# A recurrence with experts behind it: the state products of a chunk's output issued as one run, the score products as another, and a planner's table of deadlines replaced

## The chip, the cores and the metric

The kernel runs on one core of one Trainium2 chip. The metric is the device time of one execution in microseconds (us); smaller is better. The kernel before takes 564.5 us (median of three runs, 563.0 to 564.85).

Five engines matter here: TensorE (PE in the profile, its weight loads PEld), VectorE (DVE), ScalarE (ACT), GpSimd (POOL) and SyncE (SP), which issues nearly all transfers. Each engine takes its instructions in the order in which the program lists them; semaphores tie the engines together.

## The reference

Two stages. The first is a gated linear recurrence over 768 steps for 4 batches and 8 heads of 48 channels; the second is a normalised, gated feed-forward layer on all 3072 tokens (384 wide, 1536 hidden).

```python
# recurrence, for each batch and head
state = alpha[:, :, t, :, None] * state + einsum('bhd,bhe->bhde', k[:, :, t], v[:, :, t])
y[:, :, t] = einsum('bhd,bhde->bhe', q[:, :, t], state)
# experts
xn = x / sqrt(mean(x * x) + 1e-06) * rms_g
g = xn @ w_gate
out = (g * sigmoid(g) * (xn @ w_val)) @ w_out
```

## The kernel before, in words

**Chunks.** The recurrence is cut into 24 chunks of 128 tokens (6 in time for each of 4 batches; chunk `cc` is time block `cc // 4` of batch `cc % 4`). Within a chunk, with decays scanned up on DVE (line 602, two scans of 112x520), three products give the output: *scores* of queries and keys (`scores`, line 692, 48 rows of the array, heads in pairs on row halves 0 and 64), *queries with the incoming state* (again 48 rows), and *masked scores with v* (all 128 rows). `sums` (line 837, `u` below) brings keys and v together for the next state; it needs the keys turned by a transposing transfer (`k_turn`, line 633), for which there are two buffers (`kT=2`).

Every fp32 operand is held as two fp16 parts (high and low), and a product is three matmuls (high-high, high-low, low-high). Chunks 10 to 23 (`WIDE`) take the two parts of the right side side by side, 96 columns in one matmul and 48 in another, and add the two halves afterwards; chunks 4 to 9 take three matmuls of 48 columns; chunks 0 to 3 have no incoming state and use fp32.

**An output of a chunk.** It goes to one PSUM tile `y`, of which there is one (`y=1`). `output` (chunks 4 to 9, lines 811 and 820) and `output_wide` (chunks 10 to 23, lines 748 and 757) are each called twice, once for two of the four head pairs, and alternate inside: for each head pair first the state products (lines 811 or 748), then the score products (lines 820 or 757). So a chunk is four turns of state and scores. After that the output is squared, scaled, split in two fp16 parts and turned by a transfer into `xT` (line 909) for the experts; `xT` is what the experts of its group wait for.

**Experts.** The chunks form groups of 4, 2, 2, 4, 4, 4 and 4. For each group, 12 blocks of gate and value matmuls (`mm`, line 1029, columns 512 for four chunks, 256 for two; in the first group the first three blocks are cut in halves), each followed by silu (ACT, line 1040), a gate product (DVE, line 1046), and a split (ACT, then DVE, line 1059); then the output matmuls (`po`, line 1099, 384 columns, 36 for a chunk). Three PSUM tiles `mm` serve both. The weights arrive as fp64 bits and are decoded on the chip once, in the first part of the program (ACT, DVE lines 521 to 537; the first four gate/value blocks partly on PE, lines 542 and 549, through the same `y` tile).

**Who sets the order.** Every step is recorded in `Plan` with its engine, a guessed cost, what it depends on and which buffers it holds. `Plan.order` counts back from due times to a latest start for each step, then goes forward in guessed time: on each engine, of the steps that could start within 0.12 us of the earliest, it takes the one with the smallest latest start. The result is one fixed order for every engine. Due times come from the running clock of the expert blocks (`now`, moved by `GAP` at each group) and, for the chunks, from `FIRST_DUE`, `AHEAD` and `STRIDE`; `LATE` adds to the latest start of a kind of step (before, nothing for any kind).

Of the kernel before, what the change touches and what calls it, by code (L numbers as in the profile page):

```python
# [62 lines left out]
    abs=0.92, wh=0.83, pow=0.65, sc=0.8, sc32=2.3, y=0.87, y0=0.5, y32=1.85, yw=0.6, add=0.5, take=0.55, u=0.45, po=1.48,  # L63
# [20 lines left out]
class Plan:  # L84
# [9 lines left out]
    def op(self, engine, cost, fn, deps=(), use=(), due=None, lock=False, kb=0, late=0.0):  # L94

        o = dict(e=engine, c=cost, fn=fn, d=[d for d in deps if d], u=tuple(use), due=due, lock=lock,
                 kb=kb, late=late, i=len(self.ops), n=[])
# [233 lines left out]
def tile_attn_moe(  # L331
# [12 lines left out]
    nc = tc.nc  # L344
# [145 lines left out]
    def add(engine, kind, *args, **kw):  # L490
        return op(engine, COST[kind], *args, late=LATE.get(kind, 0.0), **kw)

    def decode(src, dst, name, col):
# [66 lines left out]
        o = op("SP", 0.9, load, [], [raw], kb=786, late=LATE["load"])  # L560
        o = add("ACT", "abs", fold, [o], [raw, wu])
        o = add("DVE", "shift", shift, [o], [wu], lock=True)
        o = add("DVE", "sign", sign, [o], [raw, wu], lock=True)
        o = add("DVE", "rest", rest, [o], [raw, wu], lock=True)
        if name in LOW_W:
            ps = ("y", name)
            o0 = add("PE", "wid", bring, [o], [wu, ps])
            o = add("ACT", "wh", high, [o], [wu])
            o = add("PE", "wneg", less, [o, o0], [ps])
            return add("ACT", "wl2", residue, [o], [ps])  # L570
        o = add("ACT", "wh", high, [o], [wu])
        return add("DVE", "wl", low, [o], [wu], lock=True)
# [8 lines left out]
    def attention(cc, due):  # L581

        c, b = divmod(cc, NB)
# [156 lines left out]
        def output_wide(h):  # L740
            if h == 0:
                t["y"] = tl(ps_y, [P, 2, 512], F32, "y")
            for p in (2 * h, 2 * h + 1):
                at = [t["y"][:, j, 2 * p * D : 2 * (p + 1) * D] for j in range(2)]
                for x in range(2):
                    for j in range(2):
                        r = slice(64 * j, 64 * j + D)
                        nc.tensor.matmul(  # L748
                            at[j][:, : (2 - x) * D],
                            t["q16"][r, x, p, :],  # L750
                            states[b][2][r, : 2 - x, p, :],
                            start=x == 0,
                            stop=False,
                        )
                for j in range(2):
                    for x in range(2):
                        nc.tensor.matmul(  # L757
                            at[j][:, : (2 - x) * D],
                            a_tile()[:, j, x, p, :],
                            t["v16"][:, : 2 - x, j, p, :],  # L760
                            start=False,
                            stop=x == 1,
                        )
# [36 lines left out]

        def output(h):
            if h == 0:
                t["y"] = tl(ps_y, [P, 2, 512], F32, "y")
            yps = t["y"]
            for p in (2 * h, 2 * h + 1):
                cs = slice(p * D, (p + 1) * D)
                if not first:
                    for m, (x, y) in enumerate(SPLIT):
                        for j in range(2):
                            r = slice(64 * j, 64 * j + D)  # L810
                            nc.tensor.matmul(
                                yps[:, j, cs],
                                t["q16"][r, x, p, :],
                                states[b][2][r, y, p, :],
                                start=m == 0,
                                stop=False,
                            )
                for j in range(2):
                    for m, (x, y) in enumerate(SPLIT):
                        nc.tensor.matmul(  # L820
                            yps[:, j, cs],
                            a_tile()[:, j, x, p, :],
                            t["v16"][:, y, j, p, :],
                            start=first and m == 0,
                            stop=m == 2,
                        )
# [112 lines left out]
        else:  # L939
# [6 lines left out]
            sc = add("PE", "sc", scores, [kl, ql], [key("k16"), key("q16"), at0, at1])  # L946
        if cc < OUT32:
# [5 lines left out]
        else:  # L953
# [12 lines left out]
            ins = [key("a16"), key("v16"), key("y")] + ([] if first else [key("q16")])  # L966
            kind, fn = ("yw", output_wide) if cc in WIDE else ("y0" if first else "y", output)
# [378 lines left out]
```

## Time and profile before

| | before |
|---|---|
| median of three runs | 564.5 us (563.0 to 564.85) |
| the profiled execution: span, first to last instruction | 561.7 us |
| PE busy | 523.1 us (93%), 4762 matmuls |
| DVE busy | 408.4 us (73%) |
| ACT busy | 243.7 us (43%) |
| mean granted TensorE clock | 0.976 |

The profiled execution is listed by its span alone; the median of the three runs stands 2.8 us above that span, and that is what lies around it here. A row of the timeline reads: start, length, engine, line, operation, what is written from what, count; in brackets the idle time of the engine before the row and who ended it. Equal instructions that follow each other are merged in one row, so that a row's length runs from the first one's start to the last one's end. Each matmul's own length (some 0.18 us for the small ones) is mostly pipeline: the next starts long before it ends. PE busy is therefore time covered by some matmul, and includes what is lost between two of them as long as they overlap.

### The profile page before, as it was taken

The numbers are of one execution on the slowest core, as the hardware profiler recorded it, in microseconds if no ns is written. First come the engines' busy times: TensorE is split into PE (matmuls) and PEld (weight loads), VectorE is DVE, ScalarE is ACT, GpSimd is POOL, SyncE is SP. The second block draws the span as 40 slices with busy tenths as digits, with TensorE's granted clock in tenths as the row PEclk, the third lists the DMA queues.
The fourth block names the chain that finished last, engine by engine and source line by source line (L and its number), as shares of the span: only waits on it lengthen the run. The fifth ranks groups of instructions, "written<-read, shape, count | busy, mean of one in ns | idle before, by whom it ended". The sixth has DMA issues, their size and how long they took to land.

```text
span 561.7 us, 11676 instructions
## 1 busy us (share of the span) xinstructions
PE 523.1 (93%) x4762; PEld 306.2 (55%) x4762; DVE 408.4 (73%) x741; ACT 243.7 (43%) x650; POOL 24.5 (4%) x53
## 2 busy tenths in 40 slices
PE   2877899799999999999999699999999999999995
PEld 1746644355886787544456344456554456544462
DVE  7999999999986999878885789654478643133303
ACT  2456666744344674355532264442366441133300
POOL 2101000001000001000000000000000000000000
PEclk9997999979999999999999799999999999999998
DMA  8997974463813863333324661002301001000000
GB/s 229 315 274 157 271 205 139 168 179 78 211 58 71 170 156 82 76 79 97 70 62 135 112 186 36 15 15 61 67 21 32 15 16 43 29 0 1 0 29 34
DMA packets 59693, 56.12 MB, mean 100 GB/s; under 512 B 39472, under 2 KB 54960, under 8 KB 57168
## 3 DMA queue, kind: packets, MB, share of 16 engines
q1 hardware_dynamic: 59632, 55.30, 38.3%
q8 instruction: 39, 0.64, 0.5%
q14 instruction: 22, 0.18, 0.1%
HBM read 41.26 MB, written 4.72 MB: 82 GB/s over the span
## 4 chain that ended last, share of the span: by engine, by line
PE 80%; DVE 14%; issue 2%; ACT 2%; DMA 1%; DVEq 0%; ACTq 0%
PE mm L1029 47%; PE mm_po L1099 24%; DVE att L602 3%; PE y L757 2%; PE at L692 2%; PE y L748 2%; PE at L837 1%; DVE wu_i L524 1%; DMA kT<-k 1%; PE y L820 1%; DVE a L719 1%; DVE h L1046 1%; DVE h L1059 1%; DVE x L891 1%; DVE wu_i L521 1%
## 5 line engine op out<-in xcount | busy, mean ns | idle before, releaser
L1029 PE MATMUL mm<-xT,wg 128*128 128x512 f16 (+1 forms) x1566 | 290.9, 345 | 3.5 <-ACT wg L555 1.5
L1029 PEld LDWEIGHTS <-wg 128*128 128x128 f16 x1566 | 151.6, 99 | 128.4 <-issue 4.8
L1099 PE MATMUL mm_po<-wo,h 128*128 128x384 f16 x864 | 148.1, 330 | 4.9 <-DVE h L1046 2.7
L1099 PEld LDWEIGHTS <-h 128*128 128x128 f16 x864 | 83.9, 99 | 63.1 <-issue 10.0
L1046 DVE SCALAR_TENSOR_TENSOR h<-mm,sl 128x512 f32<-128x512 f32 (+1 forms) x87 | 51.5, 592 | 42.5 <-PE mm L1029 41.8
L479 ACT ACTIVATE h<-h 128x512 f16<-128x512 f32 (+1 forms) x87 | 48.2, 554 | 78.5 <-DVE h L1046 77.8
L1059 DVE TENSOR_TENSOR h<-h,h 128x512 f16<-128x512 f32 (+1 forms) x87 | 51.4, 592 | 22.3 <-ACT h L479 22.3
L1040 ACT ACTIVATE sl<-mm 128x512 f32<-128x512 f32 (+1 forms) x87 | 45.0, 517 | 42.7 <-PE mm L1029 42.4
L602 DVE TENSOR_TENSOR_SCAN att<-att,seed 112x520 f32<-112x520 f32 x48 | 59.2, 1235 | 3.2 <-DMA att<-att 2.6
L886 POOL TENSOR_TENSOR ss<-ss,mhalf 128x1 f32<-128x1 f32 x24 | 20.2, 842 | 447.4 <-DVE ss L876 430.3
L1110 DVE TENSOR_SCALAR ob<-mm_po 128x384 f32<-128x384 f32 x24 | 13.2, 553 | 33.8 <-PE mm_po L1099 33.7
L794 ACT CAST a<-at 128x512 f16<-128x512 f32 x40 | 23.1, 583 | 20.8 <-DVE at L705 20.5
L705 DVE TENSOR_TENSOR at<-at,mask 128x512 f32<-128x512 f32 x40 | 26.1, 691 | 8.1 <-PE at L692 8.0
L797 DVE TENSOR_TENSOR a<-at,a 128x512 f16<-128x512 f32 x40 | 26.0, 682 | 0.6 <-ACT a L794 0.2
L629 DVE TENSOR_TENSOR k<-kh,k 112x512 f16<-112x512 f32 x24 | 16.4, 685 | 9.7 <-ACT k L479 9.6
L479 ACT ACTIVATE v<-v 128x384 f16<-128x384 f32 x24 | 12.5, 520 | 22.4 <-PE at L837 19.5
L479 ACT ACTIVATE k<-kh 112x512 f16<-112x512 f32 x24 | 15.0, 627 | 15.7 <-DMA kT<-k 11.4
L895 ACT ACTIVATE x<-x,ss 128x384 f16<-128x384 f32 x24 | 14.6, 610 | 14.6 <-POOL ss L886 13.6
L700 PE MATMUL at<-qp,kh 48*128 48x128 f32 x64 | 8.2, 401 | 11.4 <-DVE qp L622 10.6
L837 PE MATMUL at<-v,kT 64*48 64x48 f16 (+1 forms) x960 | 12.2, 190 | 5.7 <-DMA kT<-k 3.4
L692 PEld LDWEIGHTS <-k 48*128 48x128 f16 x480 | 13.4, 94 | 7.5 <-issue 6.3
L757 PE MATMUL y<-v,a 128*128 128x96 f16 x224 | 17.2, 197 | 0.0
(108 smaller groups left out, 455.2 us busy)
## 6 DMA issues: line engine op xcount, KB each, us to landing
att<-att SPq DMA_DIRECT2D x22, 903.0 KB, 6.0
v<-vtok SPq DMA_DIRECT2D x24, 192.0 KB, 3.1
raw_i<-w_gate SPq DMA_DIRECT2D x12, 384.0 KB, 3.9
raw_i<-w_val SPq DMA_DIRECT2D x12, 384.0 KB, 4.6
raw_o<-w_out SPq DMA_DIRECT2D x6, 768.0 KB, 4.2
out_dram<-ob SPq DMA_DIRECT2D x24, 192.0 KB, 2.2
att<-att SPq DMA_DIRECT2D x4, 227.5 KB, 3.6
att<-att SPq DMA_DIRECT2D x2, 448.0 KB, 7.1
```

What stands on the lines that cost most here:

```text
L479: nc.scalar.activation(dst, src, AF.Copy, scale=scale, accum_out=stat[:rows, col : col + 1])
L602: nc.vector.tensor_tensor_scan(x, x, start.rearrange("r g p c -> r (g p c)"), 0.0, op0=ALU.mult, op1=ALU.add)
L692: nc.tensor.matmul(o, t["k16"][r, x, p, :], t["q16"][r, y, p, :], start=m == 0, stop=m == 2,)
L705: nc.vector.tensor_tensor(t["sc"][j], t["sc"][j], mask[:, int(first)].to_broadcast([P, NP, C]), op=ALU.mult,)
L757: nc.tensor.matmul(at[j][:, : (2 - x) * D], a_tile()[:, j, x, p, :], t["v16"][:, : 2 - x, j, p, :], start=False, stop=x == 1,)
L794: nc.scalar.copy(a_tile()[:, j, 0], t["sc"][j])
L797: nc.vector.tensor_tensor(a_tile()[:, j, 1], t["sc"][j], a_tile()[:, j, 0], op=ALU.subtract)
L1029: nc.tensor.matmul(ps[:, :n], wg[:, f, x, j, kk, :], xT[:, y, kk, cs], start=i == 0, stop=i == 3 * NK - 1,)
L1040: nc.scalar.activation(t["sl"][:, :n], t[0][:, :n], AF.Silu, scale=1.0 / (S_X * S_W))
L1046: nc.vector.scalar_tensor_tensor(t["h"][:, :n], t[1][:, :n], S_H / (S_X * S_W), t["sl"][:, :n], op0=ALU.mult, op1=ALU.mult,)
L1059: nc.vector.tensor_tensor(h16_of(g, f)[:, 1, cs], t["h"][:, :n], h16_of(g, f)[:, 0, cs], op=ALU.subtract)
L1099: nc.tensor.matmul(t[i][:, :DM], h16_of(g, f)[:, x, ts], wo[:, f // 2, y, f % 2, :], start=f == 0 and m == 0, stop=f == NF - 1 and m == 2,)
```

## The change

It does three things.

1. `output` and `output_wide` go, with their two calls for a chunk. In their place stand `from_state`, all state products of the chunk in one run (16 matmuls for chunks 10 to 23, 24 for chunks 4 to 9), and `from_v`, all of the score products in one run (the same counts). The matmuls are the same in number, size and operands. Only the first one into each bank of `y` carries the start flag.
2. In the plan, the state products are a step of their own behind the queries' low part and the state's low part, and no longer behind the masked scores. `from_v` waits for them, and the next state's fp16 copy (`s16`) waits for them and no longer for the whole output. `q16` is given back after `from_state`; `y` is held from `from_state` on.
3. The due times are replaced: a table `DUE` of one number for a chunk in place of `FIRST_DUE`, `AHEAD` and `STRIDE`; other `GAP`s, a shift for each kind of step (`LATE`) and for each weight tile (`W_LATE`). So the order changes on all engines.

```diff
-GAP = [0, 14, 0, 0, 0, 0, 0]
-FIRST_DUE = [-14.0, -8.0, -2.0, 4.0]
-AHEAD = [0, 4, 8, 12, 16, 16, 16]
-STRIDE = [0, 8, 12, 12, 20, 20, 20]
-LATE = dict(load=0.0)
+GAP = [-9.2, 18.6, -4.5, -10.2, 43.4, 19.0, -49.0]
+DUE = [
+    114.5, -115.6, 73.0, 212.3, 410.5, 177.1, 435.7, 234.1, 92.3, 109.4, 118.4, 127.7, 197.1, 163.0,
...
+        def from_state():
+            wide = cc in WIDE
+            for p in range(NP):
+                for x in range(2):
+                    for y in range(1 if wide else 2 - x):
+                        for j in range(2):
+                            r = slice(64 * j, 64 * j + D)
...
+                            nc.tensor.matmul(
+                                o,
+                                t["q16"][r, x, p, :],
+                                s16,
+                                start=p == 0 and x == 0 and y == 0,
+                                stop=False,
+                                skip_group_check=True,
+                            )
+
+        def from_v():
...
             sc = add("PE", "sc", scores, [kl, ql], [key("k16"), key("q16"), at0, at1])
+            ys = add("PE", "ysw" if cc in WIDE else "ys", from_state, [ql, sl], [key("q16"), key("y")])
...
-            ins = [key("a16"), key("v16"), key("y")] + ([] if first else [key("q16")])
-            kind, fn = ("yw", output_wide) if cc in WIDE else ("y0" if first else "y", output)
-            y0 = add("PE", kind, lambda: fn(0), [l0, l1, vl, sl], ins)
-            y1 = add("PE", kind, lambda: fn(1), [y0], ins)
+            ins = [key("a16"), key("v16"), key("y")]
+            y1 = add("PE", "yvw" if cc in WIDE else "yv", from_v, [l0, l1, vl, ys], ins)
...
-        state_ops[cc] = dict(st=st, sl=sl, y=y1, dec=de, s2=s2)
+        state_ops[cc] = dict(st=st, sl=sl, y=y1 if first else ys, dec=de, s2=s2)
```

Three places of the order that comes out of it, weight loads left out.

**PE, the output of chunk 19** (`q_19`, `a_19`, `v_19` are its queries, masked scores and v; `s` is the state; lines 748 and 757 before are 771 and 792 now). Before:

```order
L1099 MATMUL mm_po_2_5425<-wo,h_4_5_4994 128x384
L748 MATMUL y_5450<-s_2210,q_19_4999 128x96
L748 MATMUL y_5450<-s_2210,q_19_4999 128x48
L757 MATMUL y_5450<-v_19_5337,a_19_5423 128x96
L757 MATMUL y_5450<-v_19_5337,a_19_5423 128x48
L748 MATMUL y_5450<-s_2210,q_19_4999 128x96
...
L757 MATMUL y_5450<-v_19_5337,a_19_5423 128x48
L1099 MATMUL mm_po_2_5425<-wo,h_4_6_5036 128x384
```

Now:

```order
L1108 MATMUL mm_po_2_5428<-wo,h_4_2_4538 128x384
L771 MATMUL y_5441<-s_1943,q_19_4951 128x96
...
L771 MATMUL y_5441<-s_1943,q_19_4951 128x48
L792 MATMUL y_5441<-v_19_5293,a_19_5414 128x96
...
L792 MATMUL y_5441<-v_19_5293,a_19_5414 128x48
L1108 MATMUL mm_po_2_5428<-wo,h_4_3_4685 128x384
```

Four turns of four and four have become one of 16 and 16. Over the program, 14 of the 20 chunks from 4 on have their two runs next to each other like this; in the six others (4, 5, 6, 9, 11 and 18) expert matmuls, scores or both stand between. State products stand directly next to a run of scores, some chunk's, in four places. Counting each step between 48-row matmuls (scores, state) and others along PE's order: 194 before, 72 now.

**PE, the sums of chunks 12, 13 and 14** (`at_2`, `at_3` from `v` and `kT`; line 837 before, 847 now), at the start of the experts of chunks 12 to 15. Before:

```order
L1099 MATMUL mm_po_3_4389<-wo,h_3_11_4128 128x384
L837 MATMUL at_2_4443<-v_12_3391,kT_3946 64x48
...
L837 MATMUL at_2_4504<-v_13_3684,kT_4250 64x48
...
L837 MATMUL at_2_4573<-v_14_3948,kT_4499 64x48
...
L1029 MATMUL mm_0_0_0_4631<-xT_3605,wg 128x512
```

Now:

```order
L1038 MATMUL mm_3_0_0_4526<-xT_3607,wg 128x512
L847 MATMUL at_2_4540<-v_13_3353,kT_3789 64x48
...
L1038 MATMUL mm_3_0_1_4593<-xT_3607,wg 128x512
L847 MATMUL at_2_4617<-v_12_3791,kT_4166 64x48
...
L1038 MATMUL mm_4_0_0_4669<-xT_3607,wg 128x512
...
L792 MATMUL y_4914<-v_16_4679,a_16_4892 128x48
L847 MATMUL at_2_4954<-v_14_3711,kT_4604 64x48
L1038 MATMUL mm_8_0_0_5006<-xT_3607,wg 128x512
```

Three sums in a row ahead of the group's first block have become three single ones inside the group; no two sums of the new order stand next to each other.

**DVE, the last gate products of the first group** (`h_0_10`, `h_0_11`; line 1046 before, 1055 now; `wu_o` and `wo` are decoded output weights, `at_1_1064` and `at_0_1105` scores of chunks 5 and 4 being masked). Before:

```order
L1046 SCALAR_TENSOR_TENSOR h_0_10_0_1254<-mm_10_0_1_1200,sl_10_0_1215 128x512
L537 TENSOR_TENSOR wo<-wu_o_1218,wo 128x768
L521 TENSOR_SCALAR wu_o_1256<-wu_o_1256 128x768
...
L1059 TENSOR_TENSOR h_0_10_1259<-h_0_10_0_1254,h_0_10_1259 128x512
L1046 SCALAR_TENSOR_TENSOR h_0_11_0_1268<-mm_11_0_1_1238,sl_11_0_1248 128x512
L537 TENSOR_TENSOR wo<-wu_o_1256,wo 128x768
L705 TENSOR_TENSOR at_1_1064<-at_1_1064,mask 128x512
```

Now:

```order
L542 SCALAR_TENSOR_TENSOR wu_o_1084<-raw_o_1019,wu_o_1084 128x768
L1055 SCALAR_TENSOR_TENSOR h_0_10_0_1131<-mm_10_0_1_1059,sl_10_0_1069 128x512
L1055 SCALAR_TENSOR_TENSOR h_0_11_0_1136<-mm_11_0_1_1091,sl_11_0_1102 128x512
L550 TENSOR_TENSOR wo<-wu_o_1053,wo 128x768
...
L1068 TENSOR_TENSOR h_0_11_1153<-h_0_11_0_1136,h_0_11_1153 128x512
L550 TENSOR_TENSOR wo<-wu_o_1084,wo 128x768
L720 TENSOR_TENSOR at_0_1105<-at_0_1105,mask 128x512
```

Ahead of the last gate product of the first group stand 169 DVE instructions before and 158 now (masks of chunks 4 and 5 among those that moved behind it); ahead of that of the second group 268 and 265, of the third 364 and 366. Chunks are also taken in another order: 13 and 14 ahead of 12, 17 ahead of 16, and 20 last of all.

More of the change, by code (lines that the diff above doesn't have):

```diff
@@ L490, in add @@
     def add(engine, kind, *args, **kw):
-        return op(engine, COST[kind], *args, late=LATE.get(kind, 0.0), **kw)
+        w = kw.get("tile")
+        late = LATE.get(kind, 0.0) + (W_LATE[w] if w is not None else 0.0)
+        return op(engine, COST[kind], *args, late=late, kind=kind, **kw)
     def decode(src, dst, name, col):
@@ L559, in decode @@
         raw, wu = ("raw", name), ("wu", name)
[L560 to L564, printed above, removed]
+        w = col - o_w
+        o = op("SP", 0.9, load, [], [raw], kb=786, late=LATE["load"] + W_LATE[w], kind="load", tile=w)
+        o = add("ACT", "abs", fold, [o], [raw, wu], tile=w)
+        o = add("DVE", "shift", shift, [o], [wu], lock=True, tile=w)
+        o = add("DVE", "sign", sign, [o], [raw, wu], lock=True, tile=w)
+        o = add("DVE", "rest", rest, [o], [raw, wu], lock=True, tile=w)
         if name in LOW_W:
             ps = ("y", name)
[L567 to L572, printed above, removed]
+            o0 = add("PE", "wid", bring, [o], [wu, ps], tile=w)
+            o = add("ACT", "wh", high, [o], [wu], tile=w)
+            o = add("PE", "wneg", less, [o, o0], [ps], tile=w)
+            return add("ACT", "wl2", residue, [o], [ps], tile=w)
+        o = add("ACT", "wh", high, [o], [wu], tile=w)
+        return add("DVE", "wl", low, [o], [wu], lock=True, tile=w)
     states = {}
@@ L738, in output32, with y_tile @@
                     )
[L740 to L744, printed above, removed]
-                for x in range(2):
[L746 to L754, printed above, removed]
+        def y_tile():
+            return tile_of(("y", cc), lambda: tl(ps_y, [P, 2, 512], F32, "y"))
@@ L755, in output_wide @@
+        def from_v():
+            wide = cc in WIDE
+            for p in range(NP):
                 for j in range(2):
                     for x in range(2):
[L757 to L763, printed above, removed]
+                        for y in range(1 if wide else 2 - x):
+                            if wide:
+                                o = y_tile()[:, j, 2 * p * D : (2 * p + 2 - x) * D]
+                                v = t["v16"][:, : 2 - x, j, p, :]
+                            else:
+                                o = y_tile()[:, j, p * D : (p + 1) * D]
+                                v = t["v16"][:, y, j, p, :]
+                            nc.tensor.matmul(
+                                o,
+                                a_tile()[:, j, x, p, :],
+                                v,
+                                start=False,
+                                stop=p == NP - 1 and x == 1,
+                                skip_group_check=True,
+                            )
+            t["y"] = y_tile()
@@ L799, in a_lo @@
             )
[L801 to L826, printed above, removed]
         def sums():
@@ L1151, in in_steps @@
         ] + [(f, 0, GROUPS[0]) for f in range(EARLY, NF)]
-    xt_ops = {cc: attention(cc, FIRST_DUE[cc]) for cc in range(GROUPS[0])}
+    xt_ops = {cc: attention(cc) for cc in range(GROUPS[0])}
     w_ops = {}
```

33 lines of the change are left out of this document (26 added, 7 removed).

## The prediction

> **What bounds the kernel now.** I read the page first, then the busy time by stretches, then the chain and the timeline where PE stops.
>
> ```profile
> span 561.7 us, 11676 instructions
> PE 523.1 (93%) x4762; PEld 306.2 (55%) x4762; DVE 408.4 (73%) x741; ACT 243.7 (43%) x650; POOL 24.5 (4%) x53
> ```
>
> PE is covered for 523.1 of 561.7 us. That average hides two parts. In the view by stretches the columns are PE, PEld, DVE, ACT and POOL busy with counts, granted clock, DMA share, GB/s:
>
> ```profile
> 0.00:217.90 217.90, 189.41 (x1983) 132.93 (x1984) 204.38 (x366) 118.15 (x335) 13.60 (x40) 0.96 0.66 174
> 217.90:555.90 338.00, 333.68 (x2784) 173.24 (x2781) 203.49 (x375) 125.57 (x315) 10.90 (x13) 0.99 0.22 53
> ...
> 47.50:68.90 21.40, 17.75 (x185) 13.18 (x186) 21.14 (x36) 13.44 (x38) 1.19 (x1) 0.94 1.00 254
> 112.50:144.10 31.60, 30.32 (x306) 18.05 (x306) 31.18 (x53) 14.38 (x35) 2.62 (x8) 0.91 0.53 150
> 167.90:186.30 18.40, 18.30 (x334) 11.80 (x336) 13.29 (x28) 7.20 (x20) 0.86 (x1) 1.00 0.43 102
> 218.00:313.60 95.60, 95.59 (x915) 51.09 (x912) 74.94 (x135) 39.13 (x103) 4.57 (x5) 1.00 0.34 86
> 313.60:319.20 5.60, 1.29 (x95) 1.14 (x94) 4.10 (x15) 2.56 (x8) 0.00 (x0) 0.75 0.87 144
> 319.20:555.90 236.70, 236.70 (x1776) 120.92 (x1772) 124.35 (x228) 83.80 (x204) 6.33 (x8) 0.99 0.15 38
> ```
>
> **The front**, up to 217.9 us (the end of the third group's last gate product), belongs to DVE: 204.4 of 217.9 us, practically all of it between 47.5 and 144. PE waits there for DVE's decoded weights and gate products. **The tail**, from 217.9 to the last matmul at 555.9, belongs to PE: 333.7 of 338.0 us, DVE little more than half busy, and all that PE lacks is one hole at 313.6 to 319.2. So a PE saving counts in full in the tail, and in the front only as far as DVE lets PE run ahead. I take the two parts one after the other.
>
> **Turns between state and score products.** The chain shows what a turn costs; here each row is a time on the path, from a run's first start to the next run's first start:
>
> ```profile
> 348.01 0.17 PE y L748 x4
> 348.18 0.24 PE y L757 x4
> 348.42 0.17 PE y L748 x4
> ...
> 349.65 11.66 PE mm L1029 x54
> ```
>
> Four turns take 349.65 − 348.01 = 1.64 us. What of it is work? The timeline has the same runs with their lengths, the groups view the length of one matmul:
>
> ```profile
> 241.69 0.24 PE L748 MATMUL y<-s,q 48*128 48x96 f16 x4
> 241.86 0.31 PE L757 MATMUL y<-v,a 128*128 128x96 f16 x4
> ...
> L748 PE MATMUL y<-s,q 48*128 48x48 f16 x112 | 10.4, 183 | 0.0
> L757 PE MATMUL y<-v,a 128*128 128x48 f16 x112 | 14.2, 185 | 0.0
> ```
>
> Of 0.24 us for four state products 0.18 is the last one's own, so it starts 0.06 us after the first; the first score product follows 0.17 after that first one, so 0.11 lies between the runs, where a step inside is about 0.02 to 0.03. For score products: 0.31 − 0.185 = 0.125, a step of 0.04, then 0.24 − 0.125 = 0.115 to the next state product. A change of kind thus costs 0.11 where a step costs 0.03 or 0.04. The new run of 16 and 16 keeps one of the seven changes inside a chunk: six go, 3 × 0.11 + 3 × 0.115 = 0.68, and six ordinary steps come, 3 × 0.03 + 3 × 0.04 = 0.21. That is **0.47 us for a chunk** (ends 0.40 and 0.53, by the step taken as 0.04 or as 0.02). Twelve chunks (12 to 23) lie in the tail: **−5.6 us**. Half of chunk 11's output, two turns or 0.82 us, lies behind 218 now and ahead of it in the new order: **−0.8**. In the tail's order state products stand next to scores three times (six changes fewer), and no sums stand next to sums (four changes more): −0.2, which I leave out. Chunks 4 to 11 save 8 × 0.47 = 3.8 us on PE too, but in the front; DVE's work covers that, and I count it at nothing.
>
> **The hole at 313.6.** PE, then SP:
>
> ```profile
> 313.00 0.59 PE L837 MATMUL at<-v,kT 64*64 64x48 f16 x49
> 314.51 0.54 PE L837 MATMUL at<-v,kT 64*64 64x48 f16 x47 [0.92 <-DVE st L855]
> 318.44 0.83 PE L837 MATMUL at<-v,kT 64*64 64x48 f16 x48 [3.40 <-DMA kT<-k]
> 319.21 4.02 PE L1029 MATMUL mm<-xT,wg 128*128 128x512 f16 x9
> 323.17 0.84 PE L692 MATMUL at<-q,k 48*128 48x128 f16 x24
> ...
> 313.66 1.25 SPq L633 DMA_TRANSPOSE kT<-k  x1
> 315.00 1.23 SPq L909 DMA_TRANSPOSE xT<-x  x1
> ```
>
> These are the sums of chunks 12, 13 and 14 in a row. There are two buffers for turned keys; the third transfer is issued at 313.66, just after the first sum has read its own, and PE stands for it until 318.44. It also waits 0.92 us for a sum's PSUM to be read. Together 4.3 us. The next nine matmuls take 323.17 − 319.21 = 3.96 us, where 54 of the kind took 11.66 (0.216 each, 1.94 for nine): the clock was at half after the hole (granted 0.75 over it), another 1.9 us with the step to the scores taken off. In the new order no two sums are neighbours, so this hole goes: **−6.2 us**. What is late next? The turned outputs of chunk 15, which the same group needs:
>
> ```profile
> xT<-x SPq DMA_TRANSPOSE x24, 2.8
> kT<-k SPq DMA_TRANSPOSE x20, 3.5
> ...
> 307.06 6.01 PE L1099 MATMUL mm_po<-wo,h 128*128 128x384 f16 x36
> ...
> 393.08 8.94 PE L1099 MATMUL mm_po<-wo,h 128*128 128x384 f16 x54
> ```
>
> Issued at 315.00 and 2.8 us on the way, they came at about 317.8, that is 10.7 us after the output's last matmul at 307.06. With the old order the group could not have begun much earlier. In the new one 72 `po` matmuls follow chunk 15's output, 72 × 0.163 (8.94 / 54, with its tail) = 11.7 us: just enough. Behind chunks 19 and 20, the last of their groups, stand 63, or 10.3 us; before, 54 were enough behind chunk 19. These margins are thin, and DVE and SP take their work in another order, so I add **+1 us** for new waits (ends 0 and 6.2).
>
> **The added wait.** `from_state` waits for the state's low part and for `y`, and behind it on PE stand expert matmuls. The closest pair is chunks 7 and 8: 18 `po` matmuls (2.9 us) between the one output and the next one's state products, and the readers of `y` are an ACT square and a DVE product of 0.55 us (below). Nothing, then; without that cover about 1 us. That `y` is held from `from_state` on costs nothing either: PE takes its list in order, and no other user stands between the two runs.
>
> **The front.** What decides is DVE's work ahead of the third group's last gate product. It ends at:
>
> ```profile
> 111.76 0.68 DVE L1046 SCALAR_TENSOR_TENSOR h<-mm,sl 128x512 f32<-128x512 f32 x1
> ...
> 217.50 0.40 DVE L1046 SCALAR_TENSOR_TENSOR h<-mm,sl 128x256 f32<-128x256 f32 x1
> ```
>
> The first of these is the first group's last: there the new order has 11 instructions fewer ahead. At the third group's the difference in kinds is one `h`, one addition, one mean and one gain more, one `q` and one decay less:
>
> ```profile
> L1059 DVE TENSOR_TENSOR h<-h,h 128x256 f16<-128x256 f32 x30 | 12.3, 412 | 0.8 <-ACT h L479 0.8
> L776 DVE TENSOR_TENSOR x<-y,x 128x384 f32<-128x384 f32 x14 | 7.7, 551 | 11.1 <-ACT x L772 11.1
> L876 DVE TENSOR_SCALAR ss<-ssq,eps 128x1 f32<-128x1 f32 x24 | 5.0, 207 | 1.6 <-ACT junk L872 1.4
> L891 DVE TENSOR_TENSOR x<-x,rg 128x384 f32<-128x384 f32 x14 | 7.7, 548 | 0.0
> L656 DVE SCALAR_TENSOR_TENSOR q<-qp,q 112x512 f16<-112x512 f32 x20 | 13.7, 685 | 0.5
> L663 DVE SCALAR_TENSOR_TENSOR gd<-dec 112x4 f32<-112x4 f32 x20 | 3.1, 153 | 0.0
> ```
>
> 0.41 + 0.55 + 0.21 + 0.55 − 0.69 − 0.15 = 0.88 us more, 0.8 of it uncovered time. So the front ends about where it did, unless DVE's idle time changes: 217.9 − 204.4 = 13.5 us, of which 18.4 − 13.3 = 5.1 lie in 167.9 to 186.3, where PE was full and DVE waited for it. In the new order PE has less to do at that place (it is ahead by the first group's 11 instructions). If those 5.1 us go, the front ends 4.3 earlier; if they stay, 0.8 later. I take **−1.5**, nearer to the middle than to the gain, since new hand-offs will idle DVE somewhere.
>
> **The sum.** −5.6 − 0.8 − 6.2 + 1.0 − 1.5 = −13.1 on a span of 561.7, so 548.6; with the 2.8 us by which the median stands above that span, **551.4 us**. From the same ends this case reaches from 546.8 (front −4.3, turns −6.4, no wait) to 556.0 (front +0.8, turns −4.8, waits 2.5).
>
> **Rivals.** *DVE idles more in the front.* Each chunk's scores, mask, split and products cross three engines, and the new order packs chunks 6 to 11 densely into the second and third group. For it: 5.1 us idle in one such stretch before. Against: between 112.5 and 144.1 DVE idled 0.4. One more such stretch: 0.8 + 5.1 instead of −1.5, +7.4, so 558.8.
>
> *A hole of the same kind elsewhere in the tail* (a group's start waiting for `xT`, or a sum for `kT`). For it: the margins of 10.3 us. Against: 54 matmuls were enough before. One hole costs 6.2 in place of the 1.0 counted: 556.6; two, 562.8.
>
> *Slower: the long runs are paced by weight loads.* Each matmul brings its own weights, and runs of score products were never longer than six.
>
> ```profile
> L757 PEld LDWEIGHTS <-a 128*128 128x128 f16 x224 | 10.2, 97 | 3.2
> ```
>
> A load takes 0.097 us; if loads stopped overlapping in a run of 16, its step would go from 0.04 to 0.097: 12 × 16 × 0.057 = +10.9 in the tail, and in the front 176 score products × 0.06 = 10.6, less the 3.8 of PE that I left uncounted, +6.8. Together +17.7 − 13.1: 569. Against it: 24 scores in 0.84 us, 0.035 each, with a load each (of 48 rows). It turns into a loss from a step of about 0.085. The Trainium skill has a rule that speaks for this (*TensorE: Matmul & The Clock Gate*, "Back-to-back issue gap"): a sustained stream of load and matmul pairs is spaced by about 81 ns at 128 columns. By that rule the tail would lose 12 × 16 × 0.041 = 7.9 and the front 176 × 0.045 − 3.8 = 4.1, and the time would be 563.4, hardly a gain; the trace so far disagrees, with 0.04 in the runs of four.
>
> *It does not do what it says.* By the order, state products stand next to scores in four places of twenty; the other 16 would save two changes each, 16 × 2 × 0.08 = 2.6 us, which I have not counted.
>
> **Chances.** Forecast 0.63; DVE idle 0.16; new holes 0.13; weight loads 0.08. Measurement tells about 0.3% (1.7 us) from no change, so faster means below 562.8, slower above 566.2. Faster: 0.63 + 0.14 + 0.10 + 0.01 = 0.88; same: 0.01 + 0.02 + 0.03 = 0.06; slower: 0.01 + 0.01 + 0.04 = 0.06. The range from 546 to 561 holds the forecast, most of the DVE case and the single hole; two holes, a worse front and the weight loads stay outside.
>
> **What would show it.** Right: PE rows of 16 state and then 16 score products, from the first start to the next expert matmul about 1.15 us instead of 1.64; PE without a wait over 1 us between 217 and 543 and a granted clock of 1.00 there; the third group's last gate product at about 216. Wrong: PE busy down by less than 6 us; DVE idle by over 17 us before that gate product; a bracket of over 3 us in the tail; a step of over 0.06 us in the long runs.

## The result, and the profile after

The changed kernel takes **544.17 us** (median of four runs, 543.04 to 544.82), the kernel before 564.08 in the same comparison (563.0 to 564.85): a ratio of **0.9645, 95% interval 0.9625 to 0.9666**. It is faster, as forecast, but by 19.9 us where 13.1 were predicted, and it lies 1.8 us below the stated range.

The page's first lines, the same ones as were read of before:

```profile
span 542.2 us, 11669 instructions
PE 507.5 (94%) x4762; PEld 299.2 (55%) x4762; DVE 405.9 (75%) x741; ACT 242.8 (45%) x650; POOL 22.8 (4%) x53
```

The number of matmuls is the same; PE is covered for 15.6 us less. The span fell by 561.7 − 542.2 = 19.5 us. The profiled run (544.2 us) stands 2.0 above its own span. For the kernel before the 2.8 was no such distance: it set the median of 564.5 against the span of another execution. Taken run by run against its own span, the time of the kernel before stands 2.1 to 2.3 above it, 2.2 in the mean.

The view by stretches, cut again at the third group's last gate product, which now ends at 214.23 (columns as in the prediction: length, then PE, PEld, DVE, ACT and POOL busy with counts, granted clock, DMA share, GB/s). The last row is the stretch in which DVE had stood for 5.1 us before:

```profile
0.00:214.23 214.23, 185.55 (x2003) 130.22 (x2004) 204.81 (x369) 120.10 (x338) 13.31 (x41) 0.93 0.69 173
214.23:536.23 322.00, 322.00 (x2761) 169.00 (x2759) 200.57 (x374) 122.69 (x312) 9.44 (x12) 1.00 0.25 58
...
167.90:186.30 18.40, 18.40 (x343) 12.28 (x341) 18.18 (x40) 10.36 (x28) 2.78 (x3) 1.00 0.57 115
```

So the front is 3.7 us shorter (217.90 to 214.23) and the tail 16.0 (338.02 to 322.00). In the tail PE has no gap left at all and the full clock throughout. In the front DVE does the same work (204.8 us against 204.4) and stands idle for 9.4 us instead of 13.5; between 167.9 and 186.3 it is busy for 18.18 us where it was 13.29.

The timeline of PE in the tail shows the new runs, and behind the second pair of them what stands where the hole was (chunk 15's output, then the group's 72 `po` matmuls without a break, then the next group; the two `po` rows are of two overlapping views of this one run of 72):

```profile
272.39 0.44 PE L771 MATMUL y<-s,q 48*128 48x96 f16 x16
272.77 0.71 PE L792 MATMUL y<-v,a 128*128 128x96 f16 x16
273.32 4.04 PE L1038 MATMUL mm<-xT,wg 128*128 128x512 f16 x18
...
292.42 0.44 PE L771 MATMUL y<-s,q 48*128 48x96 f16 x16
292.80 0.71 PE L792 MATMUL y<-v,a 128*128 128x96 f16 x16
293.35 6.82 PE L1108 MATMUL mm_po<-wo,h 128*128 128x384 f16 x41
...
296.76 8.45 PE L1108 MATMUL mm_po<-wo,h 128*128 128x384 f16 x51
305.05 1.24 PE L1038 MATMUL mm<-xT,wg 128*128 128x512 f16 x5
```

From the first start to the next expert matmul it is 273.32 − 272.39 = 0.93 us. The prediction has 1.64 for four turns and 1.15 for the new runs, but its 1.64 was read from the chain, where a row's time is not the start that the timeline gives. In the timeline the four turns of chunk 15 before start and give way at

```profile
305.51 0.24 PE L748 MATMUL y<-s,q 48*128 48x96 f16 x4
...
307.06 6.01 PE L1099 MATMUL mm_po<-wo,h 128*128 128x384 f16 x36
```

So it was 1.55 us, the saving is 0.62, and 0.93 stands against 1.55 − 0.47 = 1.08. Chunk 15's turned output is issued here on SP:

```profile
297.95 1.22 SPq L919 DMA_TRANSPOSE xT<-x  x1
```

That is 7.1 us before PE asks for it at 305.05.

### The profile page after: what moved, and what is told of

It is laid out like the page before. It is cut to its first block, busy times and chain, and to the rows that moved or that the text cites. A ratio compares the mean times of both kernels' runs of the same rounds, so it can differ in the third digit from the quotient of the medians.

```text
span 542.2 us, 11669 instructions
## 1 busy us (share of the span) xinstructions
PE 507.5 (94%) x4762; PEld 299.2 (55%) x4762; DVE 405.9 (75%) x741; ACT 242.8 (45%) x650; POOL 22.8 (4%) x53
## 4 chain that ended last, share of the span: by engine, by line
PE 80%; DVE 14%; DMA 2%; issue 2%; ACT 1%; POOL 0%; SPq 0%; DVEq 0%; ACTq 0%
PE mm L1038 45%; PE mm_po L1108 25%; PE at L707 3%; PE y L792 2%; DVE wu_i L537 2%; DVE att L617 2%; PE at L847 2%; DVE wu_i L542 1%; PE y L771 1%; DVE h L1068 1%; DVE h L1055 1%; DVE wu_i L534 1%; DMA xT<-x 1%; DMA raw_i<-w_val 1%; DVE a L734 1%
## 5 line engine op out<-in xcount | busy, mean ns | idle before, releaser
L1108 PE MATMUL mm_po<-wo,h 128*128 128x384 f16 x864 | 146.6, 328 | 1.8 <-DVE wo L550 1.8
L896 POOL TENSOR_TENSOR ss<-ss,mhalf 128x1 f32<-128x1 f32 x24 | 18.4, 768 | 433.8 <-DVE ss L886 433.8
L908 DVE SCALAR_TENSOR_TENSOR x<-x,ss,x 128x384 f16<-128x384 f32 x24 | 14.6, 610 | 6.1 <-ACT x L905 6.1
L490 ACT ACTIVATE q<-qp 112x512 f16<-112x512 f32 x20 | 12.5, 625 | 13.6 <-PE y L771 6.8
L707 PE MATMUL at<-q,k 48*128 48x128 f16 x480 | 16.9, 217 | 0.0
```

The source lines that it names most:

```text
L490: nc.scalar.activation(dst, src, AF.Copy, scale=scale, accum_out=stat[:rows, col : col + 1])
L707: nc.tensor.matmul(o, t["k16"][r, x, p, :], t["q16"][r, y, p, :], start=m == 0, stop=m == 2,)
L896: nc.gpsimd.tensor_tensor(t["ss"][:, 3:4], t["ss"][:, 2:3], mhalf, op=ALU.pow)
L1108: nc.tensor.matmul(t[i][:, :DM], h16_of(g, f)[:, x, ts], wo[:, f // 2, y, f % 2, :], start=f == 0 and m == 0, stop=f == NF - 1 and m == 2,)
```

## Experiments

For each run two numbers from its stretches are given beside the time: where the third group's last gate product ends (the front, as DVE busy plus DVE idle) and what is left to the last matmul (the tail). Before: 204.4 + 13.5 = 217.9, and 338.0. After: 204.8 + 9.4 = 214.2, and 322.0. The theory to be tested: the tail is PE's, and each change between matmuls of 48 or 64 rows and of 128 rows costs the same; the front is DVE's, its work ahead of that gate product plus its waits. The rivals are named in the expectations.

### The runs alone, in the old order

```diff
-            y0 = add("PE", kind, lambda: fn(0), [l0, l1, vl, sl], ins)
-            y1 = add("PE", kind, lambda: fn(1), [y0], ins)
+            y0 = add("PE", kind, from_state, [l0, l1, vl, sl], ins)
+            y1 = add("PE", kind, from_v, [y0], ins)
```

> The kernel before, its order on every engine and its hole at 313.6 us kept; only inside a chunk's output all state products now come first and then all score products. If a change of kind costs its 0.095 us more than a step wherever it stands and PE sets the tail, the twelve chunks there give 12 x 0.66 = 7.9 us and the front nothing, since DVE sets it: about 556.2 us, ratio 0.986. By the prediction's size (0.47 a chunk) it is 558.4, ratio 0.990. If PE sets the front as well, the eight chunks there add 5.3 us: 551, ratio 0.977. If most of the gain belongs to the new order and not to the runs, less than 3 us are gained (over 561).

Measured: 556.14 us, ratio 0.9857 (0.9831 to 0.9884). Its two stretches:

```profile
0.00:218.16 218.16, 186.69 (x1987) 131.08 (x1988) 204.67 (x366) 117.99 (x335) 13.63 (x40) 0.95 0.68 174
218.16:547.59 329.43, 325.20 (x2777) 169.58 (x2775) 202.71 (x376) 125.52 (x315) 13.20 (x13) 0.99 0.23 55
```

The tail is 8.6 us shorter (0.65 of it because four `po` matmuls now lie ahead of the cut), the front not at all, although PE is covered there for 2.7 us less (186.69 against 189.41). In the front, where turns were taken out, a wait for turned outputs came in; PE's row at the third group's start:

```profile
188.17 3.12 PE L1024 MATMUL mm<-xT,wg 128*128 128x256 f16 x27 [2.48 <-DMA xT<-x]
```

So the prediction was right to count the turns of chunks 4 to 11 at nothing, and 0.47 us for a chunk was too small.

### Four turns and two turns, in the new order

```diff
+        def from_v():
+            for p in range(0, NP, step):
+                if step < NP:
+                    state_part(range(p, p + step))
+                v_part(range(p, p + step))
```

`step` is 1 (four turns) or 2 (two turns) in the fourteen chunks where state and score products are neighbours, and all of a chunk in chunks 4, 5, 6, 9, 11 and 18, which keep their two runs.

> The kernel after with its order, but in the fourteen chunks where state and score products are neighbours (eleven of them in the tail) the output goes in four turns again, all of it in the place of the score products. If the turns cost 0.66 us a chunk: 11 x 0.66 = 7.3 us more in the tail, and 0 to 2 in the front: 551.4 to 553.4 us. By the prediction's 0.47: 549.4 to 551. If the order alone makes the gain, it stays near 545.

> The same fourteen chunks in two turns of half a chunk's output each. A turn more is two changes more. If every change has the same price, this lies a third of the way from one turn to four: 2.4 us more in the tail, 546.6 us. If the price hangs on the length of the runs (short runs of four pay more than eight), it lies nearer to one turn, at 545; if the long runs of sixteen themselves bring the gain, nearer to four turns, at 549 or more.

Measured: four turns 552.31 us, ratio 0.9793 (0.9779 to 0.9807); two turns 546.29, ratio 0.968 (0.9667 to 0.9693). The tails, first of four turns, then of two:

```profile
214.63:543.44 328.81, 328.81 (x2761) 171.91 (x2759) 201.41 (x374) 122.24 (x312) 9.42 (x12) 1.00 0.24 57
```

```profile
213.85:538.12 324.27, 324.26 (x2761) 169.98 (x2759) 200.79 (x373) 122.37 (x312) 9.41 (x12) 1.00 0.25 58
```

Over the 322.00 of after that is 6.81 us for 11 chunks and six changes each, 0.62 a chunk, and 2.27 us for two changes each, 0.21 a chunk: a third. Every change has the same price, 0.10 us net of the step that it replaces. The front moved by 0.4 us at most.

### A third buffer for the turned keys, in the old order

```diff
+            if cc == 14:
+                spare = wst.tile([P, NW], I64, tag="raw1", name="kT_14", bufs=1).bitcast(F16)
+                t["kT"] = spare[:, : 2 * NP * R].rearrange("s (x p r) -> s x p r", x=2, p=NP)
```

> The kernel before with a third buffer for the turned keys of chunk 14 alone, its order kept: the third sum no longer waits for the first to have read its own. If the whole hole hung on the buffer, the time falls by the prediction's 6.2 us to 557.9. If the turned outputs of chunk 15 are late next, as the prediction has it, their transfer is issued some 1.3 us earlier (it stood behind the keys' transfer on SP), lands at about 316.5 in place of 317.8, and PE starts the group there and not at 319.2: 2.7 us less, about 561.4, with the half clock still there.

Measured: 563.89 us, ratio 0.9995 (0.9984 to 1.0006): nothing, not even the 2.7 us that the expectation left if the turned outputs came next. SP's and PE's rows at the place:

```profile
307.12 1.27 SPq L637 DMA_TRANSPOSE kT<-k  x1
314.73 1.21 SPq L913 DMA_TRANSPOSE xT<-x  x1
```

```profile
313.51 0.59 PE L841 MATMUL at<-v,kT 64*64 64x48 f16 x49
315.02 0.64 PE L841 MATMUL at<-v,kT 64*64 64x48 f16 x48 [0.92 <-DVE st L859]
316.61 0.54 PE L841 MATMUL at<-v,kT 64*64 64x48 f16 x47 [0.95 <-DVE st L859]
319.13 3.17 PE L1033 MATMUL mm<-xT,wg 128*128 128x512 f16 x7 [1.98 <-DMA xT<-x]
```

The keys' transfer now starts 6.5 us earlier, and PE resumes at 319.13 where it was 319.21. The turned outputs of chunk 15 are late by themselves: their transfer starts at 314.73 instead of 315.00, not the 1.3 us earlier that were expected, since it was not SP that held them, and they took 4.3 us to land. DVE's rows say what held them:

```profile
313.62 0.56 DVE L1114 TENSOR_SCALAR ob<-mm_po 128x384 f32<-128x384 f32 x1 [1.51 <-PE mm_po L1103]
314.09 0.61 DVE L902 SCALAR_TENSOR_TENSOR x<-x,ss,x 128x384 f16<-128x384 f32 x1
```

The output's low part (L902) stands behind the copy of a group's result, which waits for PE's last `po`.

### Chunk 15's low part ahead of that copy: its transfer ahead of the keys', then behind it

Both kernels have the third buffer. In the first, the high part, the low part and the transfer of chunk 15 are moved ahead of the copy; in the second the transfer keeps its place in SP's list.

```diff
+        if cc == 15:
+            early.extend([xd, xl, xt])
...
+        for o in [x for x in early if ops.index(x) > cut]:
+            ops.remove(o)
+            ops.insert(cut, o)
+            cut += 1
```

> The kernel before with the third buffer for turned keys, and chunk 15's last steps (its high and low parts and their transfer) ahead of the DVE copy of the output group's result, behind which the low part had waited for PE. If the turned outputs of chunk 15 were what PE waited for at the group's start, their transfer is issued at about 313 and not 314.7, they land at about 315.6, and PE goes on when the three sums are done, near 316.7 in place of 319.1: 2.4 us less and a little of the half clock, about 561.4 us. If the two waits for the sums' PSUM grow in turn, nothing is gained (564); if all of the hole goes, 557.9.

Measured: 563.88 us, ratio 0.9994 (0.9983 to 1.0005). The first row is SP's transfer of the outputs, two microseconds earlier than with the third buffer alone, but the keys' transfer now stands behind it:

```profile
312.69 1.24 SPq L914 DMA_TRANSPOSE xT<-x  x1
313.98 1.28 SPq L638 DMA_TRANSPOSE kT<-k  x1
```

```profile
318.51 0.56 PE L842 MATMUL at<-v,kT 64*64 64x48 f16 x48 [3.43 <-DMA kT<-k]
```

The third sum waits 3.43 us for its keys, as in before (3.40). With the keys' transfer put back behind the outputs', this run does not show what the outputs alone held up; hence the second:

```diff
-            early.extend([xd, xl, xt])
+            early.extend([xd, xl])
```

> As the run with chunk 15's high and low parts ahead of the DVE copy, but its transfer keeps its place on SP behind that of chunk 14's keys, so that neither waits for the other: the keys' transfer is issued at about 307, the outputs' at about 312.7. If the hole is the later of these two transfers, PE is left with the sums' PSUM waits (0.9 us each) and goes on at about 316.7 in place of 319.2: 561.4 us, 0.995 of before, with little or no half clock behind it. If it still comes to 564, something that neither transfer explains holds PE there.

Measured: 559.48 us, ratio 0.9921 (0.9907 to 0.9934). PE, and the tail:

```profile
314.33 0.64 PE L842 MATMUL at<-v,kT 64*64 64x48 f16 x48 [0.45 <-DVE st L860]
315.92 0.54 PE L842 MATMUL at<-v,kT 64*64 64x48 f16 x47 [0.95 <-DVE st L860]
316.39 2.12 PE L1036 MATMUL mm<-xT,wg 128*128 128x512 f16 x9
```

```profile
217.90:551.90 334.00, 332.11 (x2790) 173.06 (x2788) 203.99 (x377) 125.11 (x315) 13.19 (x13) 1.00 0.21 54
```

The tail's row is cut at 217.90 and 551.90; the gate product here ends at 218.19 and the last matmul at 551.58, so the tail is 333.4 us. With both transfers early it is thus 4.6 us shorter, and the half clock is gone as well (nine `mm` in 2.05 us from start to start instead of 3.96). What stays, 1.6 us, are the waits of sums and scores for PSUM. So the hole was the later of two transfers that were equally late, and either alone gains nothing.

### The parts of the change: new steps without new deadlines, new deadlines without new steps

The first kernel is after with the due times of before (`FIRST_DUE`, `AHEAD`, `STRIDE`, the old `GAP`, no shifts); the second is after with `output` and `output_wide` back.

```diff
-            ys = add("PE", "ysw" if cc in WIDE else "ys", from_state, [ql, sl], [key("q16"), key("y")])
-            y1 = add("PE", "yvw" if cc in WIDE else "yv", from_v, [l0, l1, vl, ys], ins)
+            y0 = add("PE", kind, lambda: fn(0), [l0, l1, vl, sl], ins)
+            y1 = add("PE", kind, lambda: fn(1), [y0], ins)
```

> The two new PE steps (all state products, all score products) with the deadlines of before. The planner now sets the two steps apart in most chunks, with expert matmuls between them: per chunk still two changes of kind at the state products (from the expert matmuls to them and back), none at the score products. So the tail should save the 8 us of the turns all the same. Ahead of the fourth group's expert matmuls only 27 output matmuls (4.4 us) follow the last chunk's outputs, so the hole of before stays (6 us, or a few more), and the front is as before: about 556 to 558. If the deadlines bring nothing, it reaches 545; if the split steps themselves wait (for the state's low part ahead of queued expert matmuls), it is over 560.

> The output in four turns as two steps as before, with the new deadlines (the shifts of the two new steps given to the old ones). PE's order has no hole's place left, and chunk 11's output is whole ahead of the third group's last gate: 564.2 - 6.7 (hole and half clock) - 0.8 - 3.7 (front) = 553. Together with the split steps' 8 us that makes the 545 of after. If the front's gain needs the state products apart from the score products, the front stays at 217.9 and the time is 556.7; if the turns were the smaller part, it is under 550.

Measured: new steps alone 560.33 us, ratio 0.9931 (0.9917 to 0.9946); new deadlines alone 558.65, ratio 0.9905 (0.9891 to 0.9919). Both gained less than expected, and both lost it in the front. The stretches of the new steps alone:

```profile
0.00:223.37 223.37, 188.53 (x1953) 132.58 (x1955) 203.95 (x362) 116.99 (x333) 14.60 (x40) 0.94 0.64 168
223.37:553.27 329.90, 326.10 (x2812) 170.75 (x2811) 203.99 (x380) 126.03 (x318) 13.20 (x13) 0.99 0.23 55
```

and of the new deadlines alone:

```profile
0.00:220.31 220.31, 191.00 (x2003) 133.86 (x2004) 209.62 (x375) 121.58 (x342) 14.42 (x41) 0.98 0.66 176
220.31:550.27 329.96, 329.96 (x2761) 172.38 (x2759) 197.76 (x366) 122.18 (x308) 10.63 (x12) 1.00 0.21 52
```

The tail of the second is as the theory has it: the turns kept and the hole gone (330.0, 8.0 over after, no wait). The tail of the first is as long (329.9), but not for the reason expected. The turns are gone, and the hole of before is gone too: 90 `po` matmuls stand ahead of that group, and PE does not wait there. Instead PE waits 3.8 us in all between 236 and 242, and the clock is at half for 6.8 us from 239.4 on. Its two longest waits are

```profile
239.11 0.47 PE L760 MATMUL y<-s,q 48*128 48x96 f16 x16 [2.05 <-DVE s L686]
240.63 1.04 PE L836 MATMUL at<-v,kT 64*64 64x48 f16 x49 [1.05 <-DMA kT<-k]
```

The first is the added wait of the state products for the state's low part (L686), which the prediction put at nothing and this run's expectation named as a rival. In the order of after it does not occur; with the deadlines of before it does.

The fronts are not as expected either. With the old deadlines DVE idles 19.4 us there instead of 13.5. With the old steps DVE has 4.8 us more to do ahead of the gate product than in after (six instructions more; the planner drew chunk work forward), and idles 10.7. Neither half shortens the front; only both together do. DVE's waits go with the deadlines, though: from 160 to 200 us it is idle for 7.4 us before, 0.3 after, 1.8 with the new deadlines alone and 11.9 with the new steps alone.

### The weight tiles' shifts: left out of the new kernel, added to the old one

```diff
-W_LATE = [
-    7.6, -22.2, -83.8, -32.6, -25.0, 21.8, -13.2, -3.1, 10.2, 6.4, -38.4, 15.6, 0.1, 12.0, 9.9, 2.8,
-    38.3, 42.0,
-]
+W_LATE = [0.0] * 18
```

> The kernel after with all eighteen shifts of the weight tiles at zero; PE's list from the first step of chunk 11 on stays word for word the one of after, the front is ordered anew (the first four chunks' scores and outputs ahead of most expert matmuls, three weight tiles brought later). If the front's gain of 3.7 us over before is a matter of the deadlines of the weight tiles, it goes and the time rises to about 548. If the front is set by the sum of DVE's work alone, which is the same, it stays within 1 us of after. The tail must stay at 322 us in either case; if it changes, a wait there hung on a thin margin.

> The kernel before with nothing but the shifts of the weight tiles added to its deadlines. If these carry the front's gain alone, the third group's last gate product ends 3.7 us earlier and the time is about 560.5. If they only fit the other shifts they were searched with, the front gains nothing or loses: 564 to 580, and DVE's idle time ahead of that gate product grows from 13.5 us.

Measured: after without the shifts 565.92 us, ratio 1.004 (1.0026 to 1.0054); before with them 573.38, ratio 1.0166 (1.0153 to 1.018). The stretches of after without them:

```profile
0.00:235.49 235.49, 189.62 (x2005) 134.96 (x2006) 213.25 (x379) 121.30 (x342) 13.96 (x41) 0.93 0.65 165
235.49:557.09 321.60, 321.60 (x2759) 168.57 (x2756) 194.59 (x362) 121.28 (x308) 9.43 (x12) 1.00 0.23 53
```

The tail is the same to 0.4 us; the front alone loses 21.3 us, 8.4 of it DVE's work drawn forward and 12.8 DVE's waits. I had expected 3.7. In the old kernel the same shifts cost 9 us (front 4.0, tail 4.5), so the table is no gain by itself: it fits the other tables with which it was searched.

### DVE work added to the new kernel

```diff
+            if 4 <= cc < 20:
+                nc.vector.scalar_tensor_tensor(
+                    v_flat()[:, 1], tiles["v", cc], S_V, v_flat()[:, 0], op0=ALU.mult, op1=ALU.subtract
+                )
```

> The kernel after, with the low part of v made twice in chunks 4 to 19 (the second time writes the same values): 16 DVE instructions of about 0.55 us more, 8 of them ahead of the third group's last gate product and 8 behind it. If DVE's work sets the front and PE the tail, that gate product ends 4.4 us later (218.6), the tail keeps its 322.0, and the time is 548.6. If PE or the transfers set the front, DVE's 9.4 idle us take them up: under 546. If DVE bounded the tail too, 553.

Measured: 549.14 us, ratio 0.9731 (0.9716 to 0.9746).

```profile
0.00:218.33 218.33, 185.93 (x2004) 129.71 (x2005) 209.09 (x377) 119.95 (x338) 13.32 (x41) 0.94 0.66 170
218.33:540.04 321.71, 321.71 (x2760) 168.85 (x2757) 204.00 (x382) 121.54 (x312) 9.44 (x12) 1.00 0.26 58
```

Eight instructions ahead of the gate product put it off by 4.1 us; the eight behind it cost nothing. DVE sets the front, PE the tail.

### Scores and state products in one step

The first kernel joins them in all chunks, the second from chunk 12 on.

```diff
+            sc = ys = add("PE", "sc", lambda: (scores(), from_state()), [kl, ql, sl],
+                          [key("k16"), key("q16"), at0, at1, key("y")])
```

> The kernel after, but a chunk's scores and state products are one PE step, so that these two, which read 48 rows each, always lie side by side, and score products lie between expert matmuls of 128 rows. If only the change between few and all rows costs (0.08 to 0.095 us each), nine tail chunks that paid four changes now pay two: 9 x 0.175 = 1.6 us less in the tail, and about 542.6 us if the front holds. If the scores now wait for the state's low part, the front loses more than that: over 546, with PE waits of over 1 us ahead of scores in the first 215 us.

> The kernel after, with scores and state products joined in one PE step for chunks 12 to 23 alone; ahead of them PE's list is the one of after. Where all chunks were joined the tail took 320.7 us instead of 322.0, and what was lost was lost in the front. So the third group's last gate product should end at 214.2 as in after and the tail take 320.7: about 542.9 us, ratio 0.962. If scores wait for the state's low part now, PE waits of over 0.5 us appear behind 217 us and the time is 544 or more.

Measured: in all chunks 550.16 us, ratio 0.9757 (0.974 to 0.9775), from chunk 12 on **542.07, ratio 0.9605 (0.959 to 0.9619)**, the fastest kernel here. With all joined the tail takes 320.7 us, but the front 221.5, since 6.1 us of DVE's work was drawn ahead of its end; PE's waits ahead of scores, which the rival had, are not there but for one of 0.63 us. The stretches with all joined:

```profile
0.00:221.46 221.46, 185.51 (x2051) 132.06 (x2052) 210.87 (x379) 122.77 (x347) 12.53 (x41) 0.92 0.67 177
221.46:542.20 320.74, 319.84 (x2713) 168.73 (x2711) 194.94 (x363) 118.92 (x303) 9.73 (x12) 1.00 0.21 52
```

and with the tail alone joined:

```profile
0.00:213.57 213.57, 183.10 (x2003) 128.42 (x2004) 204.81 (x369) 120.21 (x338) 13.28 (x41) 0.94 0.70 173
213.57:534.84 321.27, 320.43 (x2761) 169.20 (x2759) 199.40 (x373) 122.35 (x312) 10.21 (x12) 1.00 0.25 59
```

The tail gains 0.73 of the 1.3 us. Most of the rest is no loss: with all joined, the 48 sums of a chunk lay ahead of the cut (2713 matmuls in the tail instead of 2761), which is 0.5 of the 1.3. Both kernels pay for one chunk whose score products, now apart, stand for their masked scores (0.90 us with all joined, 0.84 here):

```profile
333.97 0.24 PE L792 MATMUL y<-v,a 128*128 128x48 f16 x2 [0.48 <-DVE a L834]
334.57 0.60 PE L792 MATMUL y<-v,a 128*128 128x48 f16 x13 [0.36 <-DVE a L834]
```

Of the 2.1 us to after, 0.7 are in the tail and 0.7 in the front with the same DVE work. The other 0.7 cannot be placed: the profiled execution of this kernel (542.95 us) is the slowest of its five, and its span is only 1.3 us below that of after. So only the first is the edit's for certain.

## Why the prediction was wrong in size, point by point

The mechanism of the main terms held, but for half of the hole's reason. The sum was too small because two terms were undersized (the turns and the front), a third was left out as small (the rest of the tail), and one cost never came.

| term | predicted, us | measured, us | shown by |
|---|---|---|---|
| turns of chunks 12 to 23 | −5.6 (0.47 a chunk) | −7.2 to −7.4 (0.60 to 0.62) | four turns in the new order |
| chunk 11's half ahead of 218 | −0.8 | −0.8 | two turns' time in the old order |
| the hole | −6.2 | −6.5 | steps that start at a sum −4.7, at an `mm` (half clock) −1.8 |
| new waits in the tail | +1.0 | 0 | PE 322.00 of 322.00 |
| the rest of the tail | −0.2 left out | −1.4, of it 0.65 for four `po` fewer | the other 0.8: steps that start at a `po` or a score, among which fewer are changes |
| front | −1.5 | −3.7 | 217.90 to 214.23 |
| turns of chunks 4 to 11 | 0 | 0 | the runs alone: front 218.2 |
| around the span | 0 | −0.2 | 2.2 to 2.0, each run against its own span |

With 7.3 for the turns this adds up to −19.9, the measured difference. Steps are counted from a matmul's start to the next one's.

**The turns.** The price of a change was read rightly (0.115 us in every one of these traces, against 0.11 and 0.115 in the prediction). The step that takes its place was not: 0.03 and 0.04 were taken from runs of four, and in runs of sixteen it is 0.017 for state and 0.035 for score products. Six changes less six steps are 6 × 0.115 − 3 × 0.017 − 3 × 0.035 = 0.53, and the 24 steps that were inside runs already became shorter too (0.019 to 0.017 and 0.041 to 0.035, 12 each: 0.10): 0.63 in all. The prediction did not count the second. Its ends, 0.40 and 0.53, do not follow from the steps that it names either: with 0.04 and 0.02 they are 0.44 and 0.56. Its choice of the step is thus the term of the sum that failed here: 0.47 a chunk, measured 0.60 to 0.62.

**The slower rival**, long runs paced by weight loads at 0.097 us, is refuted by the same number: 0.035 a step with a load each. (The 0.035 that the prediction read for scores includes the last one's own length; from start to start they are 0.027 apart.) The rule of the Trainium skill that spoke for it (*TensorE: Matmul & The Clock Gate*, "Back-to-back issue gap") gives about 81 ns for load and matmul at 128 columns. Carried over to these score products of 96 and 48 columns, it does not hold; the measurement decides.

**The hole.** The size was right, the reason half right. "No two sums are neighbours, so this hole goes" names the keys' buffer, and a third buffer gained nothing. The prediction's next sentence, that chunk 15's turned outputs were late next, was the other half. Its figure for when they would come (317.8) was too early: it used the median of 2.8 us, and this transfer took 4.0 in before. It also did not ask why they were issued only at 315.00, where DVE's copy of the group's result had held them. In the new order both are met: sums apart, and 72 `po` matmuls behind chunk 15's output.

**The waits.** +1.0 was set aside for thin margins. The margin at chunk 15, worked out as "just enough", is 7.1 us from the issue to PE's need, against 2.9 for such a transfer's median, so 4 us wide.

**The front.** The prediction named the 5.1 us that DVE stood between 167.9 and 186.3 and said that the front would end 4.3 earlier if they went. They went (0.2 us left), and it ended 3.7 earlier. The step that failed is the choice of −1.5 between its ends, "since new hand-offs will idle DVE somewhere": no such idle time came. The runs do not show that this was bound to happen: with the new deadlines and the old steps, or the new steps and the old deadlines, the front is 2.4 to 5.5 us longer than before, and without the weight tiles' shifts 17.6 longer. I see nothing in the profile of before that would have told that this one order meets its best case; what could be read was that DVE's list ahead of that gate product grew by less than 1 us, where in two of the worse orders it is 4.8 and 8.4 us longer still. Why DVE no longer stands in that stretch is shown only so far: PE's saved turns alone do not do it (the runs in the old order), and the new deadlines with the old four turns do most of it (1.8 us idle from 160 to 200 instead of 7.4). So it is the new order; which of its moves is needed was not taken apart.

**The range.** Its lower end, 546.8, already held the front's best case (−4.3), no wait, and the turns at their upper end (−6.4). The front stayed 0.6 short of that. What carried the time below is the turns (0.9 more than that end), the rest of the tail (1.4), the hole (0.3 more) and the 2.8 us around the span, which are 2.0.

## What to carry to other kernels

Price a change by what it replaces *and* by what the neighbours become: small matmuls in a long run are cheaper by the step than in a short one. Before counting a stall as gone, list every transfer that lands at its end; when two are equally late, taking away one shows nothing. Where a static order is searched, a table's parts have no price of their own (here +9 us for the tiles' shifts alone, −4 for the steps alone, −6 for the deadlines alone, −20 for all), so the front is best forecast by one sum: the work that the bounding engine's list holds ahead of the place, and its waits.

## What the runs showed of the hardware that was not expected

- From a small 48-row matmul to a small 128-row one it is 0.112 to 0.116 us from start to start, behind runs of 4, 8 and 16 alike, and back it is 0.116 behind runs of 4 and 8; from scores to state products (both 48 rows) 0.053.
- Load and matmul pairs come 0.035 us apart in runs of sixteen score products (128 rows, 96 and 48 columns) and 0.041 in runs of four.
- The clock: in the kernel before it fell to half 1.30 us after PE's 3.40 us wait had begun (at 315.05) and stayed there for 6.83 us, although PE had been covered for a third of the 3.4 us ahead of the fall. The rows are those 3.4 us and the half clock:

```profile
312.94:316.35 3.41, 1.19 (x97) 0.92 (x96) 3.10 (x9) 1.49 (x5) 0.00 (x0) 1.00 0.40 79
316.35:323.18 6.83, 4.74 (x59) 1.93 (x60) 4.29 (x13) 1.69 (x5) 0.00 (x0) 0.50 1.16 195
```

In the old order with both transfers early, waits of 0.45, 0.95 and 0.18 us with matmuls between them left it whole:

```profile
313.00:319.40 6.40, 4.83 (x177) 2.92 (x176) 5.66 (x17) 3.42 (x11) 0.00 (x0) 1.00 0.54 134
```

The Trainium skill (*TensorE: Matmul & The Clock Gate*, "What's actually happening") has the clock halved after an idle window of about 3.4 us. The 6.83 us are two such windows, but the one ahead of the fall was not idle throughout.
